# An adaLN block on one core: the projection's quarters in another order, the gate's first product copied into the second's bank, products in another order

## The chip, the cores and the metric

The kernel runs on one core of a Trainium2 chip. The metric is the device time of one execution in microseconds (us), the median of several runs. The core has five instruction queues that run side by side and wait for each other by semaphores: TensorE (PE: matmuls; its weight loads are shown as PEld), VectorE (DVE), ScalarE (ACT), GpSimd (POOL) and SyncE (SP, which here issues DMAs). Each queue is worked off in order.

## The reference

```python
def _A_ref(x, k_cache, v_cache, wq, wo):        # B=1, Sq=Sk=2048, D=576, 32 heads, 16 kv heads, Dh=128
    W = min(4096, max(256, Sk // 4))            # 512: the last 512 keys
    q = (x @ wq) ...                            # per head
    k, v = the last W rows of the caches, each kv head for two heads
    scores = jnp.einsum("bhqd,bhkd->bhqk", q, k) * (Dh ** -0.5)
    p = _softmax(scores, axis=-1)
    o = jnp.einsum("bhqk,bhkd->bhqd", p, v)
    return o (heads side by side) @ wo
def _B_ref(x, w_gate, w_up, w_down):            # F=4608
    h = _sigmoid(x @ w_gate) * (x @ w_up)
    return h @ w_down
mod = (_silu(c) @ w_mod).reshape(c.shape[0], 6, 1, -1)
sa, ca, ga, sb, cb, gb = mod[:, 0], ..., mod[:, 5]
h = _layernorm(x) * (1 + ca) + sa
x = x + ga * _A_ref(h, ...)
h = _layernorm(x) * (1 + cb) + sb
x = x + gb * _B_ref(h, ...)
```

All tensors are float32. A_x is x.

## The kernel before, in words

**Precision and blocks.** TensorE works on numbers split into a high and a low part ("hi" and "lo", type fp32r); three matmuls make one product. A split is a ScalarE copy (hi) and a subtraction on VectorE or GpSimd (lo); names such as vh, hl, sw, hc hold both. The 2048 rows are four blocks of 512 (b = 0 to 3), each of four tiles of 128 rows (t).

**Attention** runs in two halves of two blocks, each over 32 heads. The main loop counts steps n (`N` = 512); a step makes scores (`st<-kt,qt`), four transposes (`st<-ident,pp`) and part of the output (`ot<-ptt,vs`), beside q projections for later (`qp<-hTm,wa`). On the way ScalarE writes pp and copies ptt, VectorE makes the maximum (neg) and ptt's lo part. Row sums are inverted (rs), sent through memory (rscr) and read back spread over partitions (rb); `ov<-ot,rb` is the finished output of a head. It is stored by `put_o` to oscr[half][quarter], a quarter q being eight heads. What is to be done beside this is put on a step with `at_n(n, function, ...)`. Blocks 2 and 3 are normalised in the first half: `norm_block` gives the steps for `ln_stats`, `ln_some` (12 or 13 small VectorE operations that find 1/sqrt(v), tiles ln_v, ln_y, ln_a), `ln_apply` (h), and `ln_transpose`, which first copies the last columns of h twice side by side (hd), then transposes with TensorE (`st<-ident,h`, `wo<-ident,hd`). GpSimd meanwhile prepares weights for later (`x<-x`, groups named after B_w_up and the like).

**Projection.** The output projection is multiplied by Strassen's scheme with seven products (`STAGES`) for each *visit*: a quarter q of the heads, a half p of the rows and a tile t; `PASSES` lists (q, p), four visits each; `WQ` and `WOF` say which weights are loaded for which pass. A visit loads oscr (`v_load`: `vr<-oscr`), makes three sums and a difference on GpSimd (`v_sum`: vt, vr), splits seven operands (`v_split`: vh), and runs seven stages of 12 matmuls of 288 columns with the weights wh/wscale/wshift/wgate, wb, wc, wd (loads from wosc). For the last two passes the sums are not made in the visit: they were made by `sum_o` and `sum_last` on GpSimd at attention's heads (`sx<-ov`, `sx<-sx,ov`, `ov<-ov`, `ov<-ov,sx`, for each pair of heads of the second half), stored with `put_sx` (`sscr<-sx`, `sscr<-ov`) and loaded in the visit. Which quarters are treated so stands in the table `sscr`. `late_step` prepares visit 0 in attention's last seven steps.

**FFN.** 72 steps u (two pairs of blocks, 36 slices of F), each with seven products of Strassen's scheme, seven matmuls of 512 columns each (`product`); weights sr are split to sw, the transformed inputs hc are made by `load_combo`, at the start and again at the swap of pairs (u = 36). The results lie in banks a (two), b and c (one each). Between the matmuls of a product TensorE runs matmuls of the down projection (`w<-wh,hl`), whose results VectorE adds up (`x<-w,x`). The gate is sigmoid of the sum of two products: A11 in a bank a (copied by ScalarE: `g<-a`), A12 in b (added by VectorE: `g<-b,g`). The order of the products in a step is A11, A22 of the step before, A12, S1, S2, S4, S3.

A scheduler inside the compiler places instructions where code isn't held in order (`pin`, `keep_order`). The profile's line is that of a helper (L36) for every instruction, so groups are told apart by the names of tiles.

Of the kernel before, what the change touches and what calls it, by code (L numbers as in the profile page):

```python
# [16 lines left out]
P = 128  # L17
# [27 lines left out]
def adaln_block_kernel(ctx: ExitStack, tc: tile.TileContext, x, k_cache, v_cache, wq, wo, w_gate, w_up, w_down,  # L45
# [62 lines left out]
    def keep_order(i):  # L108
        if held[0]:
            tc.keep_in_program_order(i)  # L110
# [108 lines left out]
    def ln_apply(b, t, scale_, shift_, mul, add):  # L219
# [4 lines left out]
        add.tensor_add(h, h, shift_)  # L224
        HH[b, t] = h

    def ln_transpose(b, t):
        main, tail = hTs[b]
        h = HH.pop((b, t))
        ends = wp.tile([P, 2, TAIL], F32, tag="hd", name="hd", bufs=1)  # L230
        i = nc.scalar.activation(ends, h[:, None, NC * P :].to_broadcast([P, 2, TAIL]), AF.Copy)
        keep_order(i)
        cols = slice(t * P, (t + 1) * P)
        p, pt = ps_pt(), ps_wo()
        for k in range(NC):
            nc.tensor.transpose(p[:, k * P : (k + 1) * P], h[:, k * P : (k + 1) * P], ident)
        nc.tensor.transpose(pt[:, :P], ends.rearrange("p s d -> p (s d)"), ident)
        src = p.rearrange("p (k q) -> p k q", k=NC)
        keep_order(nc.scalar.activation(main[:, :NC, cols], src, AF.Copy))
        nc.vector.tensor_sub(main[:, NC:, cols], src, f32(main[:, :NC, cols]))  # L240
        keep_order(nc.scalar.activation(tail[:, 0, cols], pt[:, :P], AF.Copy))
        nc.vector.tensor_sub(tail[:, 1, cols], pt[:, :P], f32(tail[:, 0, cols]))
# [145 lines left out]
            mod_mm(0, (3, 4), p2)  # L388
    nc.scalar.activation(shift[:, :D2], p2[0], AF.Copy)
    nc.vector.tensor_copy(shift[:, D2:], p2[1])  # L390
    ends = wp.tile([P, 2, TAIL], F32, tag="hd", name="hd", bufs=1)
    nc.scalar.activation(ends, p2[1][:, None, D2 - TAIL :].to_broadcast([P, 2, TAIL]), AF.Copy)
    pc = ps_qp()
    for k in range(NC + 1):
# [177 lines left out]
        to = oscr[half][hd // 8][:, :, hd // 2 % 4, 2 * (hd % 2) : 2 * (hd % 2) + 2]  # L572
        keep_order((nc.scalar if half * hd == H - 1 else nc.sync).dma_start(to, OT.pop((half, hd))))

    sscr = {q: dram.tile([P, TPB, 3, 4, P], F32, tag=f"sscr{q}", name=f"sscr{q}") for q in (2, 3)}
    SX = {}

    def summed(half, hd):
# [28 lines left out]
    def at_n(n, fn, *args):  # L607
        at_step.setdefault(n, []).append((fn, args))
# [74 lines left out]
    def norm_block(b, n_stats, n_apply, n_t, step, sc_, sh_, mul, add):  # L683
        for t in range(TPB):
            at_n(n_stats + t, ln_stats, b, t)
            at_n(n_apply + t * step, ln_apply, b, t, sc_, sh_, mul, add)
            at_n(n_t + t * step, ln_transpose, b, t)
        for k in range(12):
            at_n(n_stats + TPB + k, ln_some, b, False, k, k + 1, True)
        at_n(n_t - 1, new_hT, b)  # L690

    n1 = N // 2
    norm_block(2, n1 - 34, n1 - 18, n1 - 14, 2, scale, shift, nc.gpsimd, nc.gpsimd)
    norm_block(3, n1 - 26, n1 - 9, n1 - 6, 2, scale, shift, nc.gpsimd, nc.gpsimd)


    TQ = D2 - 2 * P
# [245 lines left out]
    STAGES = ((0, 0, "a", 0, 0), (4, 3, "c", 1, 1), (5, 4, "a", 0, 1), (6, 2, "c", 0, 1),  # L943
              (2, 5, "a", 1, 1), (1, 1, "b", 0, 0), (3, 6, "a", 1, 0))
    NQ = H // 8
    PASSES = (0, 0), (0, 1), (1, 1), (1, 0), (2, 0), (3, 0), (3, 1), (2, 1)
    WQ = 0, 1, 2, 3, 2
    WOF = 0, 0, 1, 1, 2, 3, 3, 4
    VISIT = [(q, p, t) for q, p in PASSES for t in range(TPB)]
    VISITS = len(VISIT)  # L950
# [57 lines left out]

    def late_step(n):
        k = n - (N - 7)  # L1010
        if k in (0, 5):
            v_load(k // 5)
        if k in (1, 2, 3):
            w_load(0, k + 1)
        if 2 <= k < 6:
            v_sum(0, k - 2)
        if k in (6, 7, 8):
            v_split(0, k - 6)

    for s in range(2):  # L1020
        at_n(N - 34 + 2 * s, w_load, 0, s)
# [42 lines left out]
        return fps.tile(shape, F32, tag=tag, name=tag, bufs=bufs)  # L1064

    B11, B21, T1, T2, B22, T3, T4 = range(7)
    HC, SW, SR, STG = {}, {}, {}, {}
    U = 2 * NF
    NG = NF // 2
# [6 lines left out]
    def stage(pair, c):  # L1076
        for i in range(2):
            stage_half(pair, c, i)

    def load_combo(pair, c, hold=False):  # L1080
        halves = STG.pop((pair, c))

        ends = hp.tile([P, TPB, 4, TQ], F32, tag="te", name="te", bufs=1)
        for i, t in enumerate(halves):
            nc.gpsimd.tensor_copy(ends[:, 2 * i : 2 * i + 2], t[:, :, None, 2 * P :].to_broadcast([P, 2, 4, TQ]))
        if c < 2:
            hc = hp.tile([P, 5, BLK], F32R, tag=f"hc{c}", name="hc", bufs=1)
        else:
            hc = fpool["h"].tile([P, 5, BLK], F32R, tag="hc", name="hc", bufs=5)
        HC[c] = hc  # L1090
        for s in range(3):
            p = fpsum("w", 4, [P, BLK])
            for i in range(TPB):
                src = halves[i // 2][:, i % 2, s * P : (s + 1) * P] if s < 2 else \
                    ends[:, i].rearrange("p q d -> p (q d)")
                m = nc.tensor.transpose(p[:, i * P : (i + 1) * P], src, ident)
                if hold:
                    pin(m)
            kind = {B11: 0, T3: 2}.get(c, 1)
            if c in (T1, T4):  # L1100
                nc.scalar.activation(hc[:, s, :], p, AF.Copy)
            else:
                nc.scalar.activation(hc[:, s, :], p, AF.Identity, bias=fcol[:, kind, s : s + 1])
            r, to = (slice(0, P), 3 + s) if s < 2 else (slice(P // 2, P), 2)
            if c in (T1, T4):
                nc.vector.tensor_sub(hc[r, to, :], p[r], f32(hc[r, s, :]))
            else:
                nc.vector.scalar_tensor_tensor(hc[r, to, :], p[r], fcol[r, kind, s : s + 1], f32(hc[r, s, :]),
                                               op0=OP.add, op1=OP.subtract)
# [3 lines left out]
    for u in range(U):  # L1113
        uses.append((u, A11))
        if u:
            uses.append((u - 1, A22))
        uses += [(u, a) for a in (A12, S1, S2, S4, S3)]
    uses.append((U - 1, A22))
    at_use = [0]

# [164 lines left out]
    def beside(v, s):  # L1285
        if v + 1 < FROM and s < 4:
            v_sum(v + 1, s)
        if s + 3 < 7:
            v_split(v, s + 3)
        elif v + 1 < VISITS:  # L1290
            v_split(v + 1, s - 4)
        if FROM <= v + 1 < VISITS and s < 3:
            v_load_sum(v + 1, s)
        if v + 2 < VISITS and s == 0:
            v_load(v + 2)
        k = WOF[v // TPB]
        if k + 1 < len(WQ):
            if v == LAST[k] and s < 4:
                w_load(k + 1, s + 3)
            elif v == LAST[k] - (6 if k == 3 else 2) and s in (1, 3, 5):  # L1300
                w_load(k + 1, s // 2)
        if DONE0 - 4 < v <= DONE0 and s in (0, 2):
            early_stats(s // 2, v - DONE0 + 3)
            park_x(s // 2, v - DONE0 + 3)
        if v < DONE0:
            return
        k = 7 * (v - DONE0) + s
        if 3 <= k < 10:
            for op in early_chain()[2 * (k - 3) : 2 * (k - 2)]:
                pin(op())  # L1310
        for t in range(TPB):
            at = k - 10 - 10 * t
            if at == 0:
                early_norm(t)
            if at in (1, 3):
                early_scale(t, at // 2)
            if 4 <= at < 8:
                early_sum(t, at - 4)
        if v == LAST[3] and s == 6:
            dctx.close()  # L1320
            fpool["s"] = ctx.enter_context(tc.tile_pool(name="fs", bufs=1, side="right", reuse_waits="tile"))
            for _ in range(4):
                load_w(True)
        if k in (36, 40, 43, 46):
            split_w()
            load_w(True)
        if k in (47, 51):
            early_stage((k - 47) // 4)
            load_combo(0, (k - 47) // 4, True)

    for s in (5, 6):
        w_load(0, s)
# [21 lines left out]
    lctx.close()  # L1354
    fpool["h"] = ctx.enter_context(tc.tile_pool(name="fh", bufs=1, reuse_waits="tile"))
    fpool["p"] = ctx.enter_context(tc.tile_pool(name="fp", bufs=1, reuse_waits="tile"))
    for c in range(2, 7):
        early_stage(c)
    for _ in range(7):
        load_sd(True)  # L1360
# [4 lines left out]
    for u in range(U + 1):  # L1365
# [21 lines left out]
        def swap(c, to):  # L1387
            if to:
                load_combo(to, c)
                if c + 2 < 7:  # L1390
                    stage(to, c + 2)


        def ahead(c):
            if u == 0:
                load_combo(0, c, True)
# [5 lines left out]
        if u < U:  # L1402
            pa, pb, pc = fpsum("a", 2, [P, BLK]), fpsum("b", 1, [P, BLK]), fpsum("c", 1, [P, BLK])
            if nxt:
                stage(nxt, 1)
            product(u, A11, B11, pa, True, (1, 3, 5) if u == U - 1 else (2, 5))
            g0 = keep(pa, "g0", 3)
            swap(B11, nxt)
            ahead(T1)
            others(0)  # L1410
        if u > 0:
            v, qa = back
# [31 lines left out]
        if u == U:  # L1444
            down_some(len(todo))
            break
        product(u, A12, B21, pb, True, downs)
        swap(B21, nxt)
        ahead(T2)
        nc.vector.tensor_add(g0, pb, g0)  # L1450
        others(1)
        product(u, S1, T1, pc, True, downs)
        swap(T1, nxt)
        ahead(B22)
        others(2)
        v1 = keep(pc, "v1", 2)
        pin(nc.scalar.activation(g0, g0, AF.Sigmoid))
        if u == U - 1:
            downs = (2, 5)
        product(u, S2, T2, pa, False, downs)  # L1460
# [59 lines left out]
```

## Time and profile before

| | |
|---|---|
| median of 3 runs | 3064.37 us (3064.32 to 3064.47) |
| the profiled execution | 3067.24 us, of it 3065.5 us span |
| mean granted TensorE clock | 0.994 |
| busy share of the span: PE, DVE, ACT, POOL | 99%, 70%, 55%, 54% |
| read from and written to memory | 394.33 MB and 173.70 MB |

The busy share counts the time in which an engine had an instruction in work; a matmul at half the clock counts as busy for twice as long. The profiled execution took 2.87 us more than the median.

### The profile page before, as it was taken

What the parts mean: (1) busy time and instruction counts of PE and PEld (TensorE: products, weight loads), DVE (VectorE), ACT (ScalarE), POOL (GpSimd) and SP (SyncE); (2) the same over time, 40 slices, a digit from 0 to 9 for tenths busy, and PEclk for the clock granted to TensorE, in tenths of its full rate; (3) what the DMA queues carried; (4) which work ended last, traced back from release to release, by engine and by line L of the source; (5) the groups of instructions that cost most, each with busy time, mean ns of one, the idle gap of its engine ahead of it and who ended that gap; (6) DMA issues with size and microseconds to landing.
All of it is one profiled execution on the core that took longest, in us unless ns stands there. A gap on an engine that the chain in (4) does not pass through costs nothing.

```text
span 3065.5 us, 49332 instructions
## 1 busy us (share of the span) xinstructions
PE 3022.1 (99%) x16639; PEld 2597.5 (85%) x16639; DVE 2147.9 (70%) x3800; ACT 1694.5 (55%) x3430; POOL 1655.5 (54%) x1544
## 2 busy tenths in 40 slices
PE   8999999999999999998999999999999999999998
PEld 6888888887888888887999998888888878888887
DVE  6666666678666666666788877666666866666667
ACT  5666667656676666554344654444444544444442
POOL 2343457635577677423555117666655666555654
PEclk9999999999999999999999999999999999999999
DMA  3677877776777767774457655555655564555453
GB/s 112 187 198 200 215 222 223 227 208 178 204 235 236 231 215 250 212 215 159 180 189 279 236 203 180 154 156 167 178 145 142 162 190 138 147 146 143 141 154 99
DMA packets 485789, 571.33 MB, mean 186 GB/s; under 512 B 52000, under 2 KB 434208, under 8 KB 476832
## 3 DMA queue, kind: packets, MB, share of 16 engines
q1 hardware_dynamic: 484400, 567.65, 61.6%
q8 instruction: 132, 2.16, 0.3%
q14 instruction: 121, 0.99, 0.1%
q10 hardware_dynamic: 1136, 0.53, 0.1%
HBM read 394.33 MB, written 173.70 MB: 185 GB/s over the span
## 4 chain that ended last, share of the span: by engine, by line
PE 90%; DVE 4%; POOL 2%; issue 1%; DMA 1%; ACT 1%; SPq 0%; POOLq 0%; ACTq 0%; DVEq 0%
PE a L36 20%; PE st L36 18%; PE qp L36 13%; PE w L36 12%; PE ot L36 11%; PE c L36 10%; PE b L36 5%; DVE x L36 1%; POOL x L36 1%; DVE neg L36 0%; PE wo L36 0%; DVE v L36 0%; DVE ptt L36 0%; DMA sr<-wsc 0%; POOL hl L36 0%
## 5 line engine op out<-in xcount | busy, mean ns | idle before, releaser
L36 DVE TENSOR_TENSOR x<-w,x 128x288 f32<-128x288 f32 x980 | 429.7, 452 | 262.0 <-PE w L36 256.9
L36 PE MATMUL a<-hc,sw 128*128 128x512 f32 x2016 | 584.9, 395 | 3.8 <-DVE v L36 3.7
L36 DVE TENSOR_REDUCE neg<-st 128x1 f32<-128x512 f32 x512 | 352.3, 688 | 272.6 <-PE st L36 271.6
L36 ACT ACTIVATE ptt<-st 128x512 fp32r<-128x512 f32 x512 | 306.1, 598 | 399.0 <-PE st L36 398.3
L36 PE MATMUL ot<-ptt,vs 128*128 128x512 f32 x1536 | 487.1, 426 | 5.4 <-DVE ptt L36 5.3
L36 PE MATMUL qp<-hTm,wa 128*128 128x512 f32 x1536 | 444.5, 398 | 4.8 <-DVE qt L36 2.4
L36 PE MATMUL st<-kt,qt 128*128 128x512 f32 x1536 | 445.0, 396 | 0.2 <-ACT pp L36 0.2
L36 DVE TENSOR_TENSOR ptt<-st,ptt 128x512 fp32r<-128x512 f32 x512 | 351.8, 687 | 126.4 <-ACT ptt L36 126.1
L36 PEld LDWEIGHTS a<-hc,sw 128*128 128x128 f32 x2016 | 355.2, 188 | 44.9 <-DVE v L36 5.2
L36 ACT ACTIVATE sw<-sr 128x384 fp32r<-128x384 f32 x504 | 257.9, 519 | 224.8 <-issue 135.4
L36 ACT ACTIVATE pp<-st,neg 128x512 f32<-128x512 f32 x512 | 350.7, 685 | 49.1 <-DVE neg L36 47.6
L36 PEld LDWEIGHTS w<-wh,hl 128*128 128x128 f32 x1776 | 298.1, 188 | 59.3 <-DVE x L36 9.2
L36 PEld LDWEIGHTS qp<-hTm,wa 128*128 128x128 f32 x1536 | 285.2, 189 | 74.3 <-DVE qt L36 8.9
L36 POOL TENSOR_TENSOR sw<-sr,sw 128x256 fp32r<-128x256 f32 x252 | 188.1, 747 | 296.5 <-ACT sw L36 281.1
L36 PEld LDWEIGHTS st<-kt,qt 128*128 128x128 f32 x1536 | 287.8, 189 | 64.3 <-ACT pp L36 0.6
L36 PE MATMUL w<-wh,hl 128*128 128x288 f32 x1776 | 329.3, 295 | 5.6 <-DVE x L36 5.2
L36 PEld LDWEIGHTS st<-ident,pp 128*128 128x128 f32 x2048 | 254.7, 140 | 73.7 <-DVE ptt L36 2.9
L36 POOL TENSOR_TENSOR x<-x 128x256 f32<-128x256 f32 (+3 forms) x334 | 246.6, 758 | 127.9 <-DMA x<-in_B_w_up_dram 68.6
L36 PE MATMUL st<-ident,pp 128*128 128x128 f32 x2048 | 308.0, 273 | 2.8 <-DVE ptt L36 2.8
L36 PE MATMUL c<-hc,sw 128*128 128x512 f32 x1008 | 304.7, 395 | 0.0
L36 PEld LDWEIGHTS ot<-ptt,vs 128*128 128x128 f32 x1536 | 254.1, 191 | 34.9 <-DVE ptt L36 8.0
L36 POOL TENSOR_TENSOR hl<-vs,hl 128x512 fp32r<-128x512 f32 x139 | 187.1, 1346 | 111.3 <-ACT hl L36 109.6
(224 smaller groups left out, 5114.3 us busy)
## 6 DMA issues: line engine op xcount, KB each, us to landing
sr<-wsc SPq DMA_DIRECT2D x504, 192.0 KB
wh<-dsc SPq DMA_DIRECT2D x144, 288.0 KB
dsc<-x SPq DMA_DIRECT2D x34, 1008.0 KB
vr<-oscr SPq DMA_DIRECT2D x32, 1024.0 KB
rb<-rscr SPq DMA_DIRECT2D x126, 256.0 KB
wsc<-x SPq DMA_DIRECT2D x36, 896.0 KB
oscr<-ov SPq DMA_DIRECT2D x63, 512.0 KB
wosc<-x SPq DMA_DIRECT2D x32, 1008.0 KB
```

The costliest lines, as they stand in the source:

```text
L36: i = got(*args, **kw)
```

## The change

It has four parts.

1. **Quarters.** The passes go over the quarters in another order: (0,0), (0,1), (3,1), (3,0), (1,0), (2,0), (2,1), (1,1). The last two passes, whose sums are made beside attention, are now quarters 1 and 2 (`sscr`), so that `sum_o`, `sum_last` and `put_sx` run at heads 8 to 23 of the second half, not at 16 to 31. In `late_step` the loads of weights, sums and splits are put one step later.
2. **Gate.** The copy of A11's bank a goes into bank b, and A12 is accumulated there by TensorE; the sigmoid reads b. The VectorE addition is gone. S1 now stands ahead of A12, and what is named by the order of inputs (`CORDER`, early loads, swaps) follows.
3. **Second normalisation.** Blocks 2 and 3 share one chain of twelve operations, six pairs on six steps, on both blocks' numbers at once; block 3's statistics start four steps earlier.
4. **hd.** The copy of h's last columns is put on the step before the transposes, in two buffers.

```diff
+    def ln_ends(b, t):
+        ENDS[b, t] = wp.tile([P, 2, TAIL], F32, tag="hd", name="hd", bufs=2)
+        keep_order(nc.scalar.activation(ENDS[b, t], HH[b, t][:, None, NC * P :].to_broadcast([P, 2, TAIL]), AF.Copy))
+
     def ln_transpose(b, t):
...
-    sscr = {q: dram.tile([P, TPB, 3, 4, P], F32, tag=f"sscr{q}", name=f"sscr{q}") for q in (2, 3)}
+    sscr = {q: dram.tile([P, TPB, 3, 4, P], F32, tag=f"sscr{q}", name=f"sscr{q}") for q in (1, 2)}
...
+            at_n(n_t + t * step - 1, ln_ends, b, t)
             at_n(n_t + t * step, ln_transpose, b, t)
-        for k in range(12):
-            at_n(n_stats + TPB + k, ln_some, b, False, k, k + 1, True)
+        if b % 2:
+            for k in range(6):
+                at_n(n_stats + TPB + k, ln_some, b, True, 2 * k, 2 * k + 2, True)
...
-    norm_block(3, n1 - 26, n1 - 9, n1 - 6, 2, scale, shift, nc.gpsimd, nc.gpsimd)
+    norm_block(3, n1 - 30, n1 - 9, n1 - 6, 2, scale, shift, nc.gpsimd, nc.gpsimd)
...
-    PASSES = (0, 0), (0, 1), (1, 1), (1, 0), (2, 0), (3, 0), (3, 1), (2, 1)
-    WQ = 0, 1, 2, 3, 2
+    PASSES = (0, 0), (0, 1), (3, 1), (3, 0), (1, 0), (2, 0), (2, 1), (1, 1)
+    WQ = 0, 3, 1, 2, 1
...
-        if k in (0, 5):
-            v_load(k // 5)
-        if k in (1, 2, 3):
-            w_load(0, k + 1)
-        if 2 <= k < 6:
-            v_sum(0, k - 2)
-        if k in (6, 7, 8):
-            v_split(0, k - 6)
+        if k in (0, 6):
+            v_load(k // 6)
+        if k in (2, 3, 4):
+            w_load(0, k)
+        if 3 <= k < 7:
+            v_sum(0, k - 3)
+        if k in (7, 8, 9):
+            v_split(0, k - 7)
...
+    CORDER = B11, T1, B21, T2, B22, T3, T4
...
-        uses += [(u, a) for a in (A12, S1, S2, S4, S3)]
+        uses += [(u, a) for a in (S1, A12, S2, S4, S3)]
...
             product(u, A11, B11, pa, True, (1, 3, 5) if u == U - 1 else (2, 5))
-            g0 = keep(pa, "g0", 3)
+            nc.scalar.activation(pb, pa, AF.Copy)
...
-        product(u, A12, B21, pb, True, downs)
-        swap(B21, nxt)
-        ahead(T2)
-        nc.vector.tensor_add(g0, pb, g0)
-        others(1)
         product(u, S1, T1, pc, True, downs)
         swap(T1, nxt)
+        ahead(T2)
+        others(1)
+        v1 = keep(pc, "v1", 2)
+        product(u, A12, B21, pb, False, downs)
+        swap(B21, nxt)
         ahead(B22)
         others(2)
-        v1 = keep(pc, "v1", 2)
-        pin(nc.scalar.activation(g0, g0, AF.Sigmoid))
+        g0 = val("g0", 3)
+        pin(nc.scalar.activation(g0, pb, AF.Sigmoid))
```

How the instructions move is shown at three places.

SyncE's queue at attention's end, before: the stores of outputs (oscr) and of the sums (sscr), the row sums' way through memory (rscr, rb), the loads of the projection's inputs (vr) and weights (wb, wd).

```order
L36 DMA oscr_3_290<-ov 512x1x256 x2
L36 DMA sscr_292<-sx 512x1x128 x2
L36 DMA rscr_280<-rs 128x4
L36 DMA rb<-rscr_280 128x512
L36 DMA sscr_292<-ov 512x1x128
L36 DMA vr<-oscr_0_283 128x2048
L36 DMA wb_15346<-wosc_352 128x2304
```

The same queue behind its next loads (two more of wb, one of vr), before:

```order
L36 DMA sscr_292<-sx 512x1x128 x2
L36 DMA oscr_3_290<-ov 512x1x256
L36 DMA sscr_292<-ov 512x1x128
L36 DMA wd_15497<-wosc_352 128x2304
L36 DMA wd_15499<-wosc_352 128x2304
```

The queue at the same place in the changed kernel:

```order
L36 DMA oscr_3_290<-ov 512x1x256
L36 DMA rscr_280<-rs 128x4
L36 DMA rb<-rscr_280 128x512
L36 DMA vr<-oscr_0_283 128x2048
L36 DMA wb_15365<-wosc_352 128x2304
L36 DMA wb_15386<-wosc_352 128x2304
L36 DMA wb_15411<-wosc_352 128x2304
L36 DMA vr<-oscr_0_283 128x2048
L36 DMA oscr_3_290<-ov 512x1x256
L36 DMA wd_15485<-wosc_352 128x2304
L36 DMA wd_15487<-wosc_352 128x2304
```

The six sscr stores of the last heads are gone from here; between the loads of wb and wd stands one store of an output.

GpSimd's queue from its last work on v (vs) to the third visit's sums, before (sx and ov: sums of heads; vt and vr: sums of a visit):

```order
L36 TENSOR_TENSOR vt<-vr 128x512
L36 TENSOR_TENSOR vr<-vr 128x4x128
L36 TENSOR_TENSOR vt<-vt,vr 128x512
L36 TENSOR_TENSOR vt<-vr,vt 128x512
L36 TENSOR_TENSOR sx<-ov 128x512
L36 TENSOR_TENSOR sx<-sx,ov 128x512
L36 TENSOR_TENSOR ov<-ov 128x4x128
L36 TENSOR_TENSOR vt<-vr 128x512
L36 TENSOR_TENSOR vr<-vr 128x4x128
L36 TENSOR_TENSOR vt<-vt,vr 128x512
L36 TENSOR_TENSOR vt<-vr,vt 128x512
L36 TENSOR_TENSOR ov<-ov,sx 128x4x128
```

And in the changed kernel:

```order
L36 TENSOR_TENSOR wa<-raw,wa 64x128
L36 TENSOR_TENSOR vs<-raw,vs 128x512
L36 TENSOR_TENSOR vt<-vr 128x512
L36 TENSOR_TENSOR vr<-vr 128x4x128
L36 TENSOR_TENSOR vt<-vt,vr 128x512
L36 TENSOR_TENSOR vt<-vr,vt 128x512
L36 TENSOR_TENSOR vt<-vr 128x512
L36 TENSOR_TENSOR vr<-vr 128x4x128
L36 TENSOR_TENSOR vt<-vt,vr 128x512
L36 TENSOR_TENSOR vt<-vr,vt 128x512
```

Nothing stands between the sums of the first two visits any more.

ScalarE's queue in one odd step u of the FFN, before (hl: hi parts for the down projection; sw: weights; `g<-a` ahead of the sw is A11's copy; `v<-c` is S1's copy; `g<-g` the sigmoid):

```order
L36 ACTIVATE hl<-v_31064 128x512
L36 ACTIVATE hl<-vs 128x512
L36 ACTIVATE g_31181<-a 128x512
L36 ACTIVATE sw<-sr 128x384 x2
L36 ACTIVATE hl<-g_30987 128x512
L36 ACTIVATE hl<-vs 128x512
L36 ACTIVATE sw<-sr 128x384
L36 ACTIVATE v_31263<-c 128x512
L36 ACTIVATE g_31181<-g_31181 128x512
```

And the same step in the changed kernel:

```order
L36 ACTIVATE hl<-v_30971 128x512
L36 ACTIVATE hl<-vs 128x512
L36 ACTIVATE b<-a 128x512
L36 ACTIVATE sw<-sr 128x384 x2
L36 ACTIVATE hl<-g_30995 128x512
L36 ACTIVATE hl<-vs 128x512
L36 ACTIVATE v_31167<-c 128x512
L36 ACTIVATE sw<-sr 128x384
L36 ACTIVATE g_31193<-b 128x512
```

The copy goes into b in the same place, S1's copy stands one sw earlier, and the sigmoid reads b.

More of the change, by code (lines that the diff above doesn't have):

```diff
@@ L225, in ln_apply @@
         HH[b, t] = h
+    ENDS = {}
+    def ln_ends(b, t):
+        ENDS[b, t] = wp.tile([P, 2, TAIL], F32, tag="hd", name="hd", bufs=2)
+        keep_order(nc.scalar.activation(ENDS[b, t], HH[b, t][:, None, NC * P :].to_broadcast([P, 2, TAIL]), AF.Copy))
     def ln_transpose(b, t):
         main, tail = hTs[b]
[L229 to L232, printed above, removed]
+        h, ends = HH.pop((b, t)), ENDS.pop((b, t))
         cols = slice(t * P, (t + 1) * P)
@@ L390, in adaln_block_kernel @@
     nc.vector.tensor_copy(shift[:, D2:], p2[1])
-    ends = wp.tile([P, 2, TAIL], F32, tag="hd", name="hd", bufs=1)
+    ends = wp.tile([P, 2, TAIL], F32, tag="hd", name="hd", bufs=2)
     nc.scalar.activation(ends, p2[1][:, None, D2 - TAIL :].to_broadcast([P, 2, TAIL]), AF.Copy)
@@ L1085, in load_combo @@
             nc.gpsimd.tensor_copy(ends[:, 2 * i : 2 * i + 2], t[:, :, None, 2 * P :].to_broadcast([P, 2, 4, TQ]))
-        if c < 2:
+        if c in (B11, T1):
             hc = hp.tile([P, 5, BLK], F32R, tag=f"hc{c}", name="hc", bufs=1)
@@ L1327, in beside @@
         if k in (47, 51):
-            early_stage((k - 47) // 4)
-            load_combo(0, (k - 47) // 4, True)
+            c = B11 if k == 47 else T1
+            early_stage(c)
+            load_combo(0, c, True)
     for s in (5, 6):
@@ L1356, in adaln_block_kernel @@
     fpool["p"] = ctx.enter_context(tc.tile_pool(name="fp", bufs=1, reuse_waits="tile"))
-    for c in range(2, 7):
+    for c in CORDER[2:]:
         early_stage(c)
@@ L1389, in swap @@
                 load_combo(to, c)
-                if c + 2 < 7:
-                    stage(to, c + 2)
+                for k in CORDER[CORDER.index(c) + 2 :][:1]:
+                    stage(to, k)
         def ahead(c):
@@ L1404, in adaln_block_kernel @@
             if nxt:
-                stage(nxt, 1)
+                stage(nxt, T1)
             product(u, A11, B11, pa, True, (1, 3, 5) if u == U - 1 else (2, 5))
-            g0 = keep(pa, "g0", 3)
+            nc.scalar.activation(pb, pa, AF.Copy)
             swap(B11, nxt)
-            ahead(T1)
+            ahead(B21)
             others(0)
```

## The prediction

> **What bounds the kernel now.** I read the page first, then TensorE's waits over the whole run, then time windows around the places where they sit, and last the timelines there.
>
> ```profile
> PE 3022.1 (99%) x16639; PEld 2597.5 (85%) x16639; DVE 2147.9 (70%) x3800; ACT 1694.5 (55%) x3430; POOL 1655.5 (54%) x1544
> ```
>
> ```profile
> PE ot L36 <- DVE ptt L36: 5.3, 7, 3.2
> PE w L36 <- DVE x L36: 5.2, 8, 1.4
> PE a L36 <- DVE v L36: 3.7, 3, 1.5
> PE b L36 <- DMA wd<-wosc: 2.3, 1, 2.3
> PE wo L36 <- ACT hd L36: 1.1, 2, 0.6
> ```
>
> TensorE is busy 99% of the span, and the change takes no matmul away. So it can win only idle time, or time at a slow clock, and lose only where something new makes TensorE wait. The other engines have room on average: 72 operations fewer on VectorE are worth nothing by themselves. The waits (total, times, longest) are few and each belongs to a place: the end of attention, the projection's start, the FFN's swap of pairs, its tail, and the second normalisation.
>
> The windows (length, busy time of PE, PEld, DVE, ACT and POOL with counts; granted clock; DMA share; GB/s) show that the slow clock costs as much as the waits:
>
> ```profile
> 1424.30:1430.50 6.20, 6.20 (x19) 5.03 (x20) 5.28 (x8) 3.80 (x9) 2.32 (x2) 0.51 1.01 426
> 1444.00:1450.00 6.00, 2.98 (x13) 2.36 (x12) 2.80 (x3) 1.17 (x2) 5.09 (x4) 0.79 0.00 0
> 1450.00:1465.00 15.00, 11.64 (x50) 10.61 (x51) 3.43 (x6) 2.09 (x5) 3.35 (x3) 0.63 0.81 316
> 1465.00:1480.00 15.00, 15.00 (x115) 15.00 (x115) 13.02 (x20) 6.82 (x12) 8.53 (x6) 1.00 0.20 72
> ```
>
> In the undisturbed last window a 288-column matmul takes 15.00/115 = 0.130 us. The two windows of 1444 to 1465 hold 63 of them, 8.2 us of work, in 21 us: **12.8 us are lost there**.
>
> **The end of attention.** TensorE's timeline, with one normal step first (st, transposes, ot), then the gap:
>
> ```profile
> 1413.39 0.86 PE L36 MATMUL st<-kt,qt 128*128 128x512 f32 x3
> 1414.10 0.60 PE L36 MATMUL st<-ident,pp 128*128 128x128 f32 x4
> 1414.45 0.96 PE L36 MATMUL ot<-ptt,vs 128*128 128x512 f32 x3
> 1415.25 0.86 PE L36 MATMUL st<-kt,qt 128*128 128x512 f32 x3
> ...
> 1424.29 1.65 PE L36 MATMUL ot<-ptt,vs 128*128 128x512 f32 x3 [3.22 <-DVE ptt L36]
> ...
> 1430.89 0.60 PE L36 MATMUL st<-ident,pp 128*128 128x128 f32 x4
> ...
> 1435.80 1.75 PE L36 MATMUL a<-wh,vh 128*128 128x288 f32 x12
> 1437.39 0.56 PE L36 MATMUL c<-wscale,vh 128*128 128x288 f32 x3
> ...
> 1456.20 2.08 PE L36 MATMUL b<-wd,vh 128*128 128x288 f32 x12 [2.32 <-DMA wd<-wosc]
> ```
>
> By start-to-start times st is 0.71, the transposes 0.35, ot 0.80 us. From 1424.29 to 1430.89 stand three ot, one st and two transposes, 3.81 us of work in 6.60: 2.8 us lost to the clock behind a gap of 3.2, so **6.0 us here**. Who holds ptt? SyncE's DMA issues, one VectorE row, the chain's piece for that load, and ScalarE:
>
> ```profile
> 1406.13 0.18 DVE L36 RECIPROCAL rs<-sum 128x4 f32<-128x4 f32 x1
> ```
>
> ```profile
> 1407.16 2.45 SPq L36 DMA_DIRECT2D sscr<-sx  x2
> 1409.97 0.62 SPq L36 DMA_DIRECT2D rscr<-rs  x1
> 1413.23 0.32 SPq L36 DMA_DIRECT2D rb<-rscr  x1
> 1413.61 0.53 SPq L36 DMA_DIRECT2D sscr<-ov  x1
> 1414.24 0.57 SPq L36 DMA_DIRECT2D vr<-oscr  x1
> ...
> 1438.15 1.89 SPq L36 DMA_DIRECT2D sscr<-sx  x2
> ...
> 1449.82 1.06 SPq L36 DMA_DIRECT2D wd<-wosc  x2
> ```
>
> ```profile
> 1414.24 6.45 DMA vr<-oscr
> ```
>
> ```profile
> 1420.71 0.63 ACT L36 ACTIVATE vh<-vr 128x512 fp32r<-128x512 f32 x1 [2.87 <-DMA vr<-oscr]
> ...
> 1422.66 0.58 ACT L36 ACTIVATE ptt<-st 128x512 fp32r<-128x512 f32 x1
> ```
>
> The projection's first vr load is issued at 1414.24, behind stores of head sums; it lands 6.45 us later; ScalarE's in-order queue has vh<-vr ahead of ptt and stands 2.87 us. Later SyncE waits for the last head's sums until 1438.15 and issues the wd weights only at 1449.82, 6.4 us before TensorE takes them.
>
> **Change, part 1: no sums at attention's end.** Its order puts no sscr store near rscr, rb and vr. The rs is ready at 1406.3, so rscr goes out about 3.5 us earlier (1409.97 to about 1406.4), rb 3.26 us behind it as before, vr right after: by that sum at 1410.1, or about 1411.7 if its buffer must first be left by the last q projection. With 6.45 us it lands at 1416.6 to 1418.2 instead of 1420.7. ScalarE's first vh goes ahead by 2.5 us or more; ptt, whose transposes start at 1420.5 in the old timeline, is held under 1 us. Of the 3.2 us I take 2.7 away, of the clock loss 1.7 of 2.8: **-4.4** (bounds -1 and -6.0). Next late there is VectorE's ov in front of ptt.
>
> In the row the clock stays half for 6.2 us after 3.22 us of idleness. [...]
>
> **Part 2: the projection's start.** The 12.8 us come from GpSimd and SyncE: the sums of the last head run ahead of visit 1's vt sums, and the wd loads stand behind the stores. In the new order GpSimd has only visit 0's and visit 1's four vt/vr operations, and SyncE only one oscr store between the vr and wd loads. That store needs the ov of the head before the last, so wd goes out before attention's last 12 ot end. TensorE wants wd0 as the fifth stage: five stages of 1.59 us (1435.80 to 1437.39), 7.9 us after the projection starts, against 6.4 us from issue to use. If the load must wait for attention's buffers it is issued at the projection's start, still 1.5 us early; bound of the miss 0 to 2. The last vh at the visits' change may wait some tenths. I take **-11.6** (bounds -7 and -12.8). The sum of the two parts is -16.
>
> **Part 3: where the sums go.** They move from heads 16 to 31 of the second half to heads 8 to 23, with GpSimd in a window that is fuller:
>
> ```profile
> 895.00:1280.00 385.00, 384.93 (x1981) 316.47 (x1980) 261.90 (x405) 260.22 (x542) 265.66 (x223) 1.00 0.73 229
> ```
>
> ```profile
> L36 POOL TENSOR_TENSOR sx<-ov x8: 1282/1292/1299, 1144.2 to 1436.8; 128x512 f32<-128x512 f32 x8
> ```
>
> Each of eight pairs of heads is four operations of 1.29 us, 5.2 us in every (1436.8 - 1144.2)/7 = 41.8. GpSimd is busy 265.66/385 = 69%, four of the eight pairs already begin in this window, and four more are 20.7 us: 74%. TensorE loses 0.07 us in these 385 although sums and weight preparation already overlap there. The stores add issues to SyncE. I take **+1.5**, bounds 0 and +5.
>
> **Part 4: second normalisation.**
>
> ```profile
> 686.00:737.00 51.00, 48.42 (x253) 37.60 (x253) 44.70 (x76) 31.76 (x76) 38.19 (x34) 1.00 0.66 174
> ```
>
> ```profile
> 695.02 1.21 DVE L36 TENSOR_TENSOR ln_a<-ln_y 128x4 f32<-128x4 f32 x1
> ```
>
> ```profile
> 697.49 0.97 PE L36 MATMUL ot<-ptt,vs 128*128 128x512 f32 x3 [0.76 <-DVE ptt L36]
> ```
>
> TensorE is idle 2.6 us of 51, and VectorE 88% busy. A chain operation on 128x4 numbers took 1.21 us; twelve of them go, the other twelve serve both blocks and run ahead of the h's. The hd copy comes a step earlier in a second buffer, so that the wo wait of 1.1 us (two times) goes. **-2.5**, bounds -4 and +1: the one joined chain could fall on a worse place.
>
> [...]
>
> **Part 5: the gate in the FFN.**
>
> ```profile
> L36 ACT ACTIVATE g<-a x144: 576/597/606, 1812.4 to 3044.7; 128x512 f32<-128x512 f32 x144
> ...
> L36 DVE TENSOR_TENSOR g<-b,g x72: 672/678/693, 1816.5 to 3042.0; 128x512 f32<-128x512 f32 x72
> ```
>
> ```profile
> 2112.75 0.58 ACT L36 ACTIVATE g<-a 128x512 f32<-128x512 f32 x1
> ```
>
> ```profile
> 2113.22 0.85 PE L36 MATMUL b<-hc,sw 128*128 128x512 f32 x3
> ...
> 2115.62 0.86 PE L36 MATMUL c<-hc,sw 128*128 128x512 f32 x3
> ```
>
> 72 of the 144 copies now write the bank b instead of SBUF, the 72 additions of 0.678 us (49 us of VectorE) go, and the sigmoid reads b. A bank-to-bank copy of 128x512 is not in the trace; the SBUF copy has 0.597, and I take that. It is on no path now. Then it is: TensorE may add A12 onto b only when the copy is done. The cover is the order of products: A12 changes place with S1. In the late case (odd u, the copy queued behind hl copies) it ends at 2113.33; A12 would start where c starts now, 2115.62: 2.3 us to spare. So 0 us. Without the exchange, the row's copy would end 0.1 us behind A12's start, at most 0.1 us times 36. The freed VectorE time is taken at the two stretches where VectorE is late: the swap of pairs (2456 to 2481: waits on v and x, the second and third rows of the waits) and the tail; an addition stood in VectorE's queue in each. I take **-1.5** (0 to -4) and **-1** (0 to -2). The exchange of early transformed inputs (T1 for B21) is neutral: as many stages, in the order of use.
>
> **Sum.** -4.4 -11.6 +1.5 -2.5 -1.5 -1 = -19.5 us. The profiled execution took 3067.24, 2.87 above the median of 3064.37; 3067.24 - 19.5 = 3047.7, less 2.87 gives **3045**. 0.2%, about what a measurement of this kernel can tell from no change, is 6.1 us: the line is 3058.2.
>
> **Rivals.**
> *A. The end of attention is only half mended* (0.17): vr still lands near 1420, or wd0 is late by 2 us and the clock stays low behind it. For it: the 6.45 us of the load do not change, and the order moves wd1's stage back. Against it: the 3.5 us won at rscr. Gain 1 + 7 and 3.5 of the other terms, 11.5: 3053.
> *B. The copy into b stalls TensorE* (0.06): slower. Place: ahead of A12, 72 times. The point is a copy more than 2.3 us later than in the row (a sigmoid or a vs wait ahead of it). If missed by 0.5 us in all: +36 -19.5 = +16.5, 3081; it ends faster than before only under 0.27 us a time. For it: ScalarE's order is fixed and one hl copy there waits for GpSimd. Against: 45% of ScalarE is free and GpSimd's queue is helped by VectorE's shorter one.
> *C. The moved sums hold ScalarE and SyncE* (0.03): GpSimd's weight preparation falls behind and 2 of the 5.2 us reach TensorE at each of eight pairs, +16; with the other terms 3064.4 - 21 + 16 is about 3059, within 0.2%. For it: 74% is a mean, and the four sums of a pair come in a bunch. Against it: the 0.07 us of part 3.
> *D. The gap only changes its name* (0.04): ptt is then held by ov, and the 12.8 us by another late vr or wd. then only normalisation and swap count, 3064.4 - 4 = 3060, within 0.2%. For it: SyncE still waits for buffers that attention leaves. Against it: in the old rows nothing but the stores stands between 1406 and 1414.
>
> **How the numbers follow.** Forecast 0.70 (3038 to 3052), A 0.17, B 0.06, C 0.03, D 0.04. Faster: 0.70 + 0.17 = 0.87; same 0.07; slower 0.06. The best ends of the terms together (6.0 + 12.8 + 4 + 4 + 2) give 28.8 us, 3036; the other end reaches over A, with both parts 1 and 2 at their poor bounds (-8) and nothing else but a gain of 0.4, to 3056. Range 3036 to 3056 leaves out B, C, D and some of the forecast's edge.
>
> **What would show it.** Right: vr issued before 1412; a gap before ot under 1 us; granted clock 1.0 from 1424 on; projection matmuls at 0.130 us from its first visit, wd issued within 2 us of the last ot; no row with TensorE waiting for ACT on b between 1830 and 3050; TensorE's idle time in the normalisation under 1 us. Wrong: a wait of product b on ACT in every u, waits of st or qp behind GpSimd's x at 900 to 1280, a gap of 2 us or more at attention's end.

## The result, and the profile after

| | before | changed |
|---|---|---|
| median, first comparison | 3064.35 us (4 runs, 3064.25 to 3064.47) | 3050.64 us (4 runs, 3046.3 to 3053.7) |
| ratio | | 0.9954, 95% interval 0.9937 to 0.9971 |
| profiled execution | 3067.24 us | 3053.7 us |
| mean granted clock | 0.994 | 0.996 |

The changed kernel is 13.7 us faster; its runs lie 7.4 us apart. The profiled execution is the slowest of the four, 13.5 us under that of before. TensorE's waits over the whole run (total, times, longest) show what went and what came:

```profile
PE qp L36 <- DVE qt L36: 6.0, 4, 2.4
PE w L36 <- DVE x L36: 5.2, 8, 1.4
PE a L36 <- DVE v L36: 4.3, 4, 1.4
PE wo L36 <- DMA wm<-in_w_mod_dram: 2.4, 1, 2.4
PE ot L36 <- DVE ptt L36: 1.8, 4, 1.0
```

In the profile of before the wait for qt was

```profile
PE qp L36 <- DVE qt L36: 2.4, 3, 1.0
```

The waits for wd and hd are gone, that for ptt fell from 5.3 to 1.8 us. The waits for x and v, which belong to the FFN, hardly changed (8.9 us together before, 9.5 now). The waits for qt grew from 2.4 to 6.0 us; two long ones, of 2.43 and 1.78 us, are new. The load of w_mod at the very start waits 2.4 us, 1.1 in the profile of before; nothing of the change touches it.

**Attention's end.** TensorE's timeline there (start, duration; in brackets the idle time and what ended it), then SyncE's:

```profile
1424.82 0.60 PE L36 MATMUL st<-ident,pp 128*128 128x128 f32 x4
1426.39 0.96 PE L36 MATMUL ot<-ptt,vs 128*128 128x512 f32 x3 [0.97 <-DVE ptt L36]
...
1432.17 3.06 PE L36 MATMUL ot<-ptt,vs 128*128 128x512 f32 x12
```

```profile
1410.68 0.32 SPq L36 DMA_DIRECT2D rscr<-rs  x1
1412.13 0.32 SPq L36 DMA_DIRECT2D rb<-rscr  x1
1412.56 0.37 SPq L36 DMA_DIRECT2D vr<-oscr  x1
...
1432.74 0.53 SPq L36 DMA_DIRECT2D oscr<-ov  x1
1433.37 2.24 SPq L36 DMA_DIRECT2D wd<-wosc  x2
```

From the transposes ahead of the gap to the last twelve ot it took 1432.17 - 1424.82 = 7.35 us. For before the same two rows are

```profile
1420.47 0.60 PE L36 MATMUL st<-ident,pp 128*128 128x128 f32 x4
...
1432.90 3.07 PE L36 MATMUL ot<-ptt,vs 128*128 128x512 f32 x12
```

12.43 us: 5.1 us are won. Measured from those transposes, vr is now issued 12.3 us ahead of them, before 6.2 us. The gap of 0.97 us did not lower the clock (1.00 from 1426.30 to 1430.00). And the projection's start runs at a clock of 1.00 (a window of the changed kernel: length, busy time of PE, PEld, DVE, ACT, POOL with counts, granted clock, DMA share, GB/s):

```profile
1440.00:1465.00 25.00, 25.00 (x190) 25.00 (x189) 20.61 (x31) 10.72 (x18) 12.49 (x9) 1.00 0.48 186
```

190 matmuls in 25 us are 0.132 us each, against 63 in 21 us before: of 12.8 us lost, 0.2 are left.

**A new loss at 1042.** TensorE, VectorE and SyncE in the changed kernel:

```profile
1042.06 1.27 PE L36 MATMUL qp<-hTm,wa 128*128 128x512 f32 x3 [2.43 <-DVE qt L36]
```

```profile
1020.57 0.18 DVE L36 RECIPROCAL rs<-sum 128x4 f32<-128x4 f32 x1
...
1039.73 1.07 DVE L36 TENSOR_TENSOR ov<-ot,rb 128x512 f32<-128x512 f32 x1 [2.93 <-DMA rb<-rscr]
...
1041.32 0.68 DVE L36 SCALAR_TENSOR_TENSOR qt<-qp,qt 128x512 fp32r<-128x512 f32 x1
```

```profile
1023.24 1.25 SPq L36 DMA_DIRECT2D oscr<-ov  x2
1024.54 2.46 SPq L36 DMA_DIRECT2D sscr<-sx  x2
1027.10 0.87 SPq L36 DMA_DIRECT2D rscr<-rs  x1
...
1029.08 1.01 SPq L36 DMA_DIRECT2D dsc<-x  x2
1032.27 0.32 SPq L36 DMA_DIRECT2D rb<-rscr  x1
```

The same place before:

```profile
1021.77 0.43 SPq L36 DMA_DIRECT2D rscr<-rs  x1
...
1023.53 2.46 SPq L36 DMA_DIRECT2D dsc<-x  x2
1026.08 0.76 SPq L36 DMA_DIRECT2D rb<-rscr  x1
```

The row sums rs are ready at 1020.75, but rscr goes out at 1027.10, behind the stores of a pair of heads; before it followed rs by 1.55 us. Its rb follows at 1032.27. Two weight stores of a megabyte each (dsc) stand ahead of rb, but they did so before too. rb lands 7.4 us after its issue; ov stands 2.93 us for it in VectorE's queue, and qt behind ov. Of the 6.35 us between rs and rscr, 2.5 are SyncE's wait for GpSimd's sum (total, times, longest, 1015 to 1042); the rest is mostly the issue of the four stores:

```profile
SPq L36 <- POOL ov L36: 2.5, 1, 2.5
```

SyncE's other long waits in that stretch, for rscr's landing and for dsc, come behind this rscr or ahead of the pair's stores. The stores stand ahead of rscr at each of the eight pairs, where rscr follows rs by 3.4 to 7.5 us. Only here is the whole way too long: ov begins 19.0 us after rs, 2.93 of them waited for, where 15 to 16 us are usual without a wait.

What the place costs is seen in one window of each kernel, before first:

```profile
1000.00:1060.00 60.00, 60.00 (x310) 49.29 (x309) 41.35 (x64) 42.92 (x88) 46.65 (x38) 1.00 0.68 216
```

```profile
1000.00:1060.00 60.00, 57.57 (x288) 47.04 (x287) 37.41 (x58) 39.31 (x80) 49.66 (x41) 0.97 0.69 211
```

22 of 310 matmuls fewer in 60 us, at 60/310 = 0.194 us each: 4.3 us, of it 2.4 idle time and the rest clock.

### The profile page after: what moved, and what is told of

Its sections match the earlier page's. It is cut to its first block, busy times and chain, and to the rows that moved or that the text cites. A ratio compares the mean times of both kernels' runs of the same rounds, so it can differ in the third digit from the quotient of the medians.

```text
span 3051.9 us, 49183 instructions
## 1 busy us (share of the span) xinstructions
PE 3014.0 (99%) x16639; PEld 2591.7 (85%) x16639; DVE 2110.7 (69%) x3716; ACT 1691.8 (55%) x3430; POOL 1654.8 (54%) x1544
## 4 chain that ended last, share of the span: by engine, by line
PE 91%; DVE 3%; POOL 2%; issue 1%; DMA 1%; ACT 1%; SPq 0%; POOLq 0%; DVEq 0%; ACTq 0%
PE a L36 21%; PE st L36 18%; PE qp L36 13%; PE w L36 12%; PE ot L36 11%; PE c L36 10%; PE b L36 5%; DVE x L36 1%; POOL x L36 1%; PE wo L36 0%; DVE v L36 0%; POOL hl L36 0%; POOL vs L36 0%; DVE neg L36 0%; DMA rb<-rscr 0%
## 5 line engine op out<-in xcount | busy, mean ns | idle before, releaser
L36 DVE TENSOR_TENSOR sw<-sr,sw 128x256 fp32r<-128x256 f32 x252 | 179.1, 711 | 143.9 <-ACT sw L36 143.8
```

What stands on the lines that cost most here:

```text
L36: i = got(*args, **kw)
```

## The experiments

**One part at a time** (each part on the kernel before), and the changed kernel again. The first run holds `PASSES`, `WQ`, `sscr` and `late_step`:

```diff
...
+    sscr = {q: dram.tile(...) for q in (1, 2)}
...
+    PASSES = (0, 0), (0, 1), (3, 1), (3, 0), (1, 0), (2, 0), (2, 1), (1, 1)
+    WQ = 0, 3, 1, 2, 1
...
```

> Before with the quarters part alone (PASSES, WQ, sscr, late_step). Theory: this part holds nearly the whole gain: about -18 us between 1400 and 1480, and about +4 us near 1042, where the moved stores make rb late, so about -14 us, 3050 us, with a spread between runs as wide as the whole change has (some 7 us). Rival: the gain at attention's end needs the freed engines of the other parts; then this part gives -10 us or less.

3051.71 us (3047.49 to 3053.89), 0.9958 (0.9945 to 0.997) of before: 12.9 us, of the 13.8 that the whole change gives in this comparison; the interval reaches from 9.2 to 16.9. The profiled execution is its fastest, 3047.49, and there the place near 1040 has a gap of 1.48 us at full clock, 58.52 of the 60 us from 1000 busy at 1.00, where the changed kernel's slowest run lost 4.3. Between 1440 and 1465 it has 190 matmuls at a clock of 1.00 (before: 92 at 0.73) without the other parts, so the rival of shared credit falls.

The second holds the copy into b, the exchange of A12 and S1 and `CORDER`:

```diff
...
-            g0 = keep(pa, "g0", 3)
+            nc.scalar.activation(pb, pa, AF.Copy)
...
-        nc.vector.tensor_add(g0, pb, g0)
...
```

> Before with the gate part alone (copy into b, products in another order, inputs' order). Theory: no wait of TensorE on the copy, 72 additions off VectorE's path; the two stretches where VectorE is late hardly shorten: 0 to -1.5 us, and runs within 0.5 us of each other. Rival: the additions were the cause of the waits at the swap of pairs and in the tail: -4 us or more. Rival: the copy stalls product A12: +5 us or more.

3066.53 us, 1.0006 (0.9997 to 1.0015): no change that can be told. Both rivals fall. Its runs lie 6.4 us apart, not within 0.5; the 21 of before in the same comparison lay 6 us apart too, so the first four runs of before, 0.2 us apart, don't show how far its runs can lie from each other.

The third joins the chain and moves the hd copy:

```diff
...
+            at_n(n_t + t * step - 1, ln_ends, b, t)
...
+        if b % 2:
+            for k in range(6):
+                at_n(n_stats + TPB + k, ln_some, b, True, 2 * k, 2 * k + 2, True)
...
```

> Before with the joined chain and the earlier hd copy alone. Theory: the two waits for hd and the chain's own waits go, 2.5 us, but the h operations now meet GpSimd near 689 and a wait of 1.8 us for qt with its clock loss comes in: -0.7 us in all. Rival: that wait belongs to the quarters part and does not come here: -2.5 us.

3062.77 us, 0.9992 (0.9984 to 1.0001): 1.9 us by the medians, with an interval that reaches no change. The wait for qt comes here too, 2.00 us at 688.44, so it belongs to this part; in this profile the clock stayed at 1.00 behind it.

> The changed kernel once more, for the spread of its runs (3046.3 to 3053.7 so far). Theory: the late rb near 1042 is there in some runs and absent in others, so that a profile of a faster run shows less than 1 us lost between 1000 and 1060, and one of a slower run about 4.5. Rival: the spread lies at the start (the first load of w_mod) or elsewhere, and the loss near 1042 is the same in all profiles.

3050.8 us (3047.73 to 3053.8), 0.9952 (0.9939 to 0.9966). The one profile is again of the slowest run and again has the loss near 1042 (a gap of 2.29 us, clock 0.60 for the next 4 us), so by itself it doesn't tell the two apart. The other traces do in part. Every trace of a kernel with the stores at this place has the gap: 2.11 us in the fastest run with the h held (below), with a clock of 0.61 in the 4.1 us from 1035.40; 2.41 in the run with late_step as before, with 0.97 over the 60 us from 1000; 1.48 in the fastest run of the quarters part, with 1.00 over the same 60; and 1.49 in the fastest without the exchange. So the late rb is not absent in faster runs, as the theory had it; its length varies, and the clock behind it was full in one of these traces and not in others. How much of the spread that makes is not shown.

**Taking the new waits away.** First the stores:

```diff
-                    m += 1 if b == NBLK - 1 else 2
+                    m += 3
                     at_late(m, put_o, half, hd - 1)
                     at_late(m, put_o, half, hd)
-                    at_late(m, put_sx, hd, (0, 1))
-                    at_late(m + 2, sum_last, hd)
-                    at_late(m + 3, put_sx, hd, (2,))
+                    at_late(m + 2, put_sx, hd, (0, 1))
+                    at_late(m + 1, sum_last, hd)
+                    at_late(m + 4, put_sx, hd, (2,))
```

> The changed kernel with the sums' work after their first step put later: outputs stored one step later, sscr<-sx three steps later, the last difference and its store two steps later, so that SyncE finds GpSimd's sums done. Theory: the wait near 1042 (2.4 us, 3.5 to 4.5 with the clock) comes because SyncE stands behind the stores and rscr and rb go out late; it goes: 3047 us, about -4 against the changed kernel, and its runs lie within 3 us. Rival: rb lands late because the DMA queues are full with weights and sums at that place; then the wait stays over 1.5 us.

(The last difference itself stays on its old step, but for the last pair; its store comes two steps later.) 3045.77 us, 0.9936 (0.9924 to 0.9949): 5.0 us under the changed kernel's 3050.8 in the other comparison, and as far under the run with late_step as before (3050.77, below) in the same one, with runs only 1.35 us apart (3045.47 to 3046.82). SyncE at the same place, and TensorE's window:

```profile
1017.60 0.33 SPq L36 DMA_DIRECT2D rscr<-rs  x1
1020.02 1.25 SPq L36 DMA_DIRECT2D oscr<-ov  x2
...
1022.45 2.54 SPq L36 DMA_DIRECT2D dsc<-x  x2
1025.08 1.39 SPq L36 DMA_DIRECT2D rb<-rscr  x1
1026.51 2.82 SPq L36 DMA_DIRECT2D sscr<-sx  x2
```

```profile
1000.00:1060.00 60.00, 60.00 (x310) 49.17 (x309) 41.41 (x64) 41.89 (x86) 51.56 (x41) 1.00 0.75 250
```

rscr goes out first and rb ahead of sscr; all 310 matmuls are back, at a higher DMA rate (250 against 211 GB/s). rb is still issued behind the two dsc stores, and its ov begins 8.5 us after rb's issue (7.5 in the changed kernel), without a wait. So it was the place in the queue, not the load of the DMA engines by itself, that made the difference. Most of the spread is gone with this wait.

Then the h:

```diff
-        nc.vector.tensor_scalar(h, xs[b][:, t, :], mv[:, t, 0:1], y[:, t : t + 1], op0=OP.subtract, op1=OP.mult)
+        i = nc.vector.tensor_scalar(h, xs[b][:, t, :], mv[:, t, 0:1], y[:, t : t + 1], op0=OP.subtract, op1=OP.mult)
+        pin(i)
```

> The changed kernel with ln_apply's VectorE operation held in program order, so that the four h of block 2 are spread over eight steps. Theory: the wait of 1.8 to 2.0 us for qt near 689 comes because two h, lengthened from 0.58 to 1.3 and 1.5 us by GpSimd, stand ahead of qt; it goes and the time falls by 2 to 3 us, 3048. Rival: the h come so late that the transposes wait for them: 3052 or more.

3048.96 us, 0.9945 (0.9933 to 0.9958), 1.8 us under the changed kernel's 3050.8 in another comparison, and under the 3050.77 with late_step as before in the same one. The two intervals overlap; the profile shows the step. VectorE's h and qt in the changed kernel, then with the h held:

```profile
684.58 1.32 DVE L36 TENSOR_SCALAR h<-x,mv,ln_y 128x576 f32<-128x576 f32 x1
...
687.41 1.48 DVE L36 TENSOR_SCALAR h<-x,mv,ln_y 128x576 f32<-128x576 f32 x1
688.82 0.68 DVE L36 SCALAR_TENSOR_TENSOR qt<-qp,qt 128x512 fp32r<-128x512 f32 x1
```

```profile
683.46 0.69 DVE L36 SCALAR_TENSOR_TENSOR qt<-qp,qt 128x512 fp32r<-128x512 f32 x1
687.88 0.55 DVE L36 TENSOR_SCALAR h<-x,mv,ln_y 128x576 f32<-128x576 f32 x1
694.00 0.57 DVE L36 TENSOR_SCALAR h<-x,mv,ln_y 128x576 f32<-128x576 f32 x1
```

Spread out, an h takes 0.55 and 0.57 us, where the two beside GpSimd's h (684.14 to 690.16 in the changed kernel) took 1.32 and 1.48, and qt comes ahead of them. The loss near 1040 is still there in this run: a gap of 2.11 us, with a clock of 0.61 from 1035.40 to 1039.50.

**The cover of the copy.** The exchange of A12 and S1 taken back (the order of the products and of their inputs goes back with this line):

```diff
...
-        uses += [(u, a) for a in (S1, A12, S2, S4, S3)]
+        uses += [(u, a) for a in (A12, S1, S2, S4, S3)]
...
```

> The changed kernel without the exchange of A12 and S1 (products and inputs in the old order), A12 accumulated onto the copied bank. Theory: the cover of 2.3 us is what keeps the copy off the path; without it TensorE waits for the copy in the 36 odd steps some 0.1 to 0.3 us each, and in more at the swap: +4 to +12 us against the changed kernel, 3055 to 3063, with rows of product b waiting for ACT. Rival: other products' order hides it anyway: within 1.5 us of 3051.

3059.46 us (eleven runs, 3055.15 to 3065.48), 0.9982 (0.9973 to 0.999): 8.7 us over the changed kernel's 3050.8. One odd step, ScalarE and TensorE:

```profile
2093.94 0.58 ACT L36 ACTIVATE b<-a 128x512 f32<-128x512 f32 x1
```

```profile
2094.18 0.40 PE L36 MATMUL a<-hc,sw 128*128 128x512 f32 x1
2094.57 0.97 PE L36 MATMUL b<-hc,sw 128*128 128x512 f32 x3
```

b starts 0.39 us behind the last a, where c behind the last b has 0.23 in the same trace (2096.87 to 2097.10), and its three take 0.11 longer than the usual 0.86: 0.27 us in each of 36 odd steps would be 9.7 us. In the changed kernel the copy stands in the same place and its bank is wanted later:

```profile
2099.24 0.58 ACT L36 ACTIVATE b<-a 128x512 f32<-128x512 f32 x1
```

```profile
2102.23 0.86 PE L36 MATMUL b<-hc,sw 128*128 128x512 f32 x3
```

It ends at 2099.82, 2.4 us ahead. The exchange is the part of the gate change that matters.

**late_step as before:**

```diff
-        if k in (7, 8, 9):
-            v_split(0, k - 7)
+        if k in (6, 7, 8):
+            v_split(0, k - 6)
```

(and the other three lines alike)

> The changed kernel with late_step as before (loads, sums and splits of visit 0 one step earlier). Theory: the gain at attention's end comes from the stores and sums taken away there, and the scheduler places visit 0's work by readiness: within 1.5 us of the changed kernel. Rival: the later step is what lets ptt go ahead of vh: at least 2 us more idle time before ot near 1426.

3050.77 us, 0.995 (0.9936 to 0.9963): nothing. The gain at attention's end is that of the queues.

**Both mendings together**, and the same without the gate part:

> The changed kernel with the stores later and the h pinned, both as in the runs before. Theory: the two new waits are separate, so the gains add: 5 us by the stores and 1.8 by the h below 3050.8, about 3044, and the runs lie within 2 us. Rival: the wait at the second normalisation and the one near 1042 share a cause (SyncE's queue); then nothing is added and it stays at 3045.8.

3044.64 us (3044.45 to 3045.22), 0.9935 (0.9921 to 0.9949): 6 us under the changed kernel, with runs 0.8 us apart. Beside the stores alone it is 1.1 us, less than the 1.8 expected, and the kernel before was 1.0 us faster in this comparison too (3063.93 against 3064.94): measured against it, the stores alone gain 19.2 us and both together 19.3. By the times nothing is shown to be added. That the two waits are separate is shown by the profiles: with the stores alone TensorE still idles 1.9 of the 51 us from 686, with the h alone the gap near 1040 stays, and with both the two are gone:

```profile
1000.00:1060.00 60.00, 60.00 (x308) 49.10 (x307) 40.33 (x63) 41.25 (x86) 51.59 (x42) 1.00 0.74 252
686.00:737.00 51.00, 50.84 (x276) 41.34 (x275) 39.49 (x70) 34.23 (x83) 35.98 (x33) 1.00 0.73 189
```

> The same without the gate part (A11 copied to SBUF, 72 additions on VectorE, old order of products). Theory: the gate part is worth nothing, since no wait of TensorE came from the additions: within 1 us of the run beside it. Rival: the additions do cost at the swap and in the tail: at least 2 us more. Rival: the gate part costs, as the median of its run alone (1.9 us above) would say: at least 1.5 us less.

3044.62 us (3043.28 to 3046.85), 0.9935 (0.9923 to 0.9948). With the disturbances gone, the two medians are 0.02 us apart (the runs of each 0.8 and 3.6): no worth of the gate part can be told, and both rivals fall.

## Why the prediction was right, and where its sizes were off

**Parts 1 and 2** held. At attention's end 5.1 us were won (4.4 forecast, bound 6.0), at the projection's start 12.6 (11.6, bound 12.8). rscr moved up as reckoned; rb followed it 1.45 us later instead of 3.26, so vr went out earlier still. The remaining gap of 0.97 us is the wait for ptt foreseen "under 1 us". wd is not waited for. Rivals A and D fall. The load vr was issued at 1412.56, not before 1412 as the signs had it, in a profile that ran over 4 us late by then; measured from the transposes it is early.

**Part 3 was mis-sized**: 4.3 us in the profiled run for a forecast of 1.5. The step that failed is the argument from the rows: sums beside weight preparation cost 0.07 us in the old stretch, so eight pairs would cost little more. Those rows held stores that came late too, but none so late that ov waited. GpSimd's busy share, the price I put first, was not the limit; SyncE's queue was, at one pair of heads of eight. The bound of 5 held it. Rival C named SyncE among those held, but as a loss at each of eight pairs: it was one place. Of the signs of being wrong, a wait of qp did come, behind a late rb and not behind GpSimd's x.

**Part 4 was mis-sized**: 1.9 us alone, of 2.5, with the interval of 0.9984 to 1.0001, and in the changed kernel's profile only 0.7 us less idle time: 1.9 us stay idle instead of the "under 1 us" foreseen. The chain's and hd's waits went as said; the term left out that the h then run 4 us earlier (687.84 before, 683.48 now, both the first h of block 2), so that three of them stand ahead of qt at 688.82. Before, the four ran in a bunch beside GpSimd too (687.84 to 693.67), but behind that qt, at 685.86. "The one joined chain could fall on a worse place" was the bound for it, not the number.

**Part 5** was right in its nought for the copy, and the cover of 2.3 us is shown by the run without it. Without the exchange the prediction would have had at most 0.1 us in each of 36 steps, 3.6 us; it was 8.7, since in the step shown TensorE begins b 0.16 us late and its three matmuls take 0.11 us longer. The 2.5 us for the swap and the tail were wrong: the additions stand in VectorE's queue there, but the waits for x and v (5.2 and 4.3 us now, 5.2 and 3.7 before) did not come from them. Rival B falls at this cover; that the copy can hold TensorE is shown where the cover is 0.

**The sum** by the profile is -5.1 -12.6 +4.3, -0.7 at the normalisation (idle time between 686 and 737: 51 - 48.42 before, 51 - 49.12 in the changed kernel) and -0.6 at the swap (its four waits: 5.1 and 4.5 us), and +1.3 at the w_mod load: about -13.4, where the two profiled executions differ by 13.5. That the total time (13.7 us gained, 19.5 forecast) lay this near came from both sides: parts 1 and 2 gave 1.7 us more than forecast, parts 3 to 5 gave 6.5 less, and the w_mod load, which the change doesn't touch, cost 1.3. The sum is that of a slow run of the changed kernel; its median is 3 us lower, and which terms are smaller there is not shown.

## What to carry to other kernels

Work that is moved off a crowded place takes its DMA issues with it: look at what is queued behind them on SyncE at the new place, and how long the small transfers there may wait, not only at the busy share of the engine that computes. An accumulation that replaces an addition puts a copy on TensorE's path; one other product between copy and accumulation was worth 8.7 us here, and the addition that it saved nothing. A wide spread between runs came with a wait that had full clock behind it in one trace (1.48 us) and half in others (2.11 and 2.43 us): taking the wait away left runs 1.35 and 0.8 us apart instead of 7.4 (3.6 without the gate part).

## What the runs showed of the hardware

The clock's answer to a gap was not the same each time. In the traces of before and of the changed kernel it was half for 3.41 us or for twice that (but for the stretch that runs into the end), and these times begin whole multiples of 3.41 us apart: before, at 1423.58, 1447.47 and 1457.71, 7 and 3 multiples; in the changed kernel, at 690.95 and 1042.53, 103 multiples. Here are stretches of that length, two of them behind each other, at the two gaps of 2.43 and 1.78 us in the changed kernel (the second number is TensorE's busy time as the profile models it, the granted clock is the last but two):

```profile
1039.12:1042.53 3.41, 0.98 (x5) 0.50 (x4) 2.79 (x5) 0.78 (x2) 1.48 (x1) 1.00 0.89 206
1042.53:1045.94 3.41, 3.41 (x12) 2.71 (x11) 1.51 (x4) 1.72 (x5) 0.00 (x0) 0.50 0.44 133
...
687.54:690.95 3.41, 1.63 (x8) 1.18 (x7) 3.41 (x5) 0.94 (x3) 3.33 (x3) 1.00 0.53 158
690.95:694.36 3.41, 3.41 (x12) 2.76 (x11) 1.95 (x4) 2.16 (x6) 3.33 (x4) 0.50 1.01 290
```

And at the gap of 2.00 us in the normalisation part:

```profile
686.57:689.98 3.41, 1.54 (x7) 1.26 (x8) 3.41 (x5) 0.78 (x2) 3.33 (x3) 1.00 0.93 245
689.99:693.40 3.41, 3.41 (x21) 2.87 (x20) 2.33 (x5) 2.41 (x6) 3.33 (x4) 1.00 0.86 231
```

In the changed kernel's rows 2.43 and 1.78 us of idleness have a clock of 0.50 behind them, in those of the normalisation part 1.87 us have 1.00. Cut into such stretches, the two whole traces have this: every one at full clock in which TensorE was idle for 1.78 us or more was followed by one at half clock, and none with 1.46 us or less was (1.46 before, from 2478.30, with 1.00 behind it). What decides between 1.46 and 1.87 us is not shown. A stretch of 3.41 us at 0.50 loses about 1.7 us of work, an estimate from these rows' clock (3.41 x 0.50).

The gap of 3.22 us before falls across the border of two stretches: 2.51 us of it in the one from 1420.17, 0.70 in the next, and the clock was 0.50 for two, from 1423.58 to 1430.41. In both traces full clock came back only behind a stretch at half with 0.55 us of idleness or less; those with 0.70 to 0.88 were followed by another at half.

For the nine runs of the changed kernel the record has the mean granted clock: 0.996 in those of 3053.45 to 3053.8 us, 0.997 from 3049.69 to 3051.6, 0.998 from 3046.3 to 3048.11. So the slower runs are those with more time at half clock; 0.002 of 3050 us are 6.1 us, near the whole spread of 7.4. In which stretches the faster runs lost less, those near 1042 or those of the start, is not shown run by run.
